# Attention into hash-routed experts on one core: where the token list stands, how rows are written, and which engine builds the tables

## The chip, the cores and the metric

The kernel runs on one core of a Trainium2 chip. The core has five engines that run their own instruction streams in order and meet through semaphores: PE (TensorE, matrix products), DVE (VectorE), ACT (ScalarE), POOL (GpSimd) and SP (SyncE, which here only sends DMAs). The metric is device time in microseconds (us), lower is better; three runs of the kernel before gave 185.52, 185.73 and 187.29, median 185.73.

## The reference, cut to what matters

Two blocks follow each other. The first is attention with polynomial features, for 4 batches, 4 heads, 1088 positions and head size 32:

```python
def phi(x):                      # S1, S2: 8 x 32
    a = np.einsum('rd,bhsd->bhsr', S1, x)
    b = np.einsum('rd,bhsd->bhsr', S2, x)
    return np.einsum('bhsi,bhsj->bhsij', a, b).reshape(*x.shape[:-1], 64)
q_p, k_p = phi(q), phi(k)
kv  = np.einsum('bhsf,bhsd->bhfd', k_p, v)
z   = np.sum(k_p, axis=2)
x   = einsum(q_p, kv) / (einsum(q_p, z) + 1e-6)    # -> 4352 tokens x 128
```

The second sends every token to one of 8 experts by its id, `token_ids * 2654435761 % 8`, and computes `relu(x @ w1[e]) @ w2[e]` with w1 of 128 x 1024 and w2 of 1024 x 128.

## The kernel before

**Order.** All five engines run in the order in which the program issues work (line 92). So where a call stands in the source is where its instructions stand on each engine, and an engine that waits holds up what is queued behind it.

**Attention.** Each of the four batches goes through the same steps. PE turns k and q (`turned_all`, L451 to L465; ACT copies the result out), multiplies them with the sketch matrices (`s_products`), ACT copies the first factors (`first_copied`), and DVE multiplies out the 64 features of q and of k (`features`, L510, two halves of four position tiles each). PE turns the features of q (`q_turned`, L559; ACT and DVE copy two quarters each), sums kv over the positions (`kv_products`, L532: eight tiles of 128 positions and a tail of 64), ACT copies it into a block diagonal m (`kv_diagonal`), and PE multiplies turned features with m (`x_products`, `x_tail_products`). A column of ones beside v gives the denominator. DVE inverts it (`denominators`), POOL scales the rows (`x_main`, `x_tail`, L597 to L612) and a DMA writes them to the DRAM tensor `x_rows`, in one piece of 512 KB for the main part and one of 32 KB for the tail. v is copied into place by POOL (`values`). The loop over b (L756) handles the products of batch b together with the features of batch b + 1; the fourth batch's products follow the loop (L812 to L821).

**Routing.** Between these steps the routing is spread out. DVE finds each token's expert, its rank among that expert's tokens and the expert's place in an order by size. `route_slots` (L365) turns that into a slot for each token, and splits the slot number into a tile number and a row number (st). `route_rows` and `route_tiles` (L403 to L411) build one-hot tables by comparing st with counters; `route_tiles_p` scales one of them on ACT. `route_list` (L416) is 34 products on PE that give, for each slot, the token in it, and `route_end` (L432) makes the two index tables, get for fetching and put for storing. In the third batch (b = 2) the list stands after kv, and the end after the products with the sketch matrices.

**Experts.** Each expert has two groups of slots: an early one of 256 tokens from the first two batches (groups 0 to 7) and a late one of 320 down to 271 columns (groups 8 to 15). `fetch_tile` (L665) gathers 128 rows by an indirect DMA of POOL; `paced` (L672) puts a small copy of the indices on DVE in front of it, so that it is not issued early. Chunks 0 and 1 are turned on PE (`bring`, L683). Later ones are split by DVE into halves of 16 bits (`turn_in`, L690), transposed by a DMA of SP, and put together again by DVE (`join_in`, L698). A group is eight products of the first layer (`layer1`, L831, four PSUM banks in turn, ACT clears the even ones and DVE the odd ones) interleaved with the eight of the second layer (`layer2`, L840) of the group before. At full speed it takes PE about 6.9 us for 256 columns. Results leave by ACT's copies, transposing DMAs (`turn_out`), DVE's joins (`join_out`) and indirect stores of POOL (`scatter`). The last group is handled in two parts, and its rows are turned on PE (`out_rows`).

**Work beside the products.** A list written out by hand (`beside`, L953 to L994) says after which product (group, chunk of the hidden layer) which of these steps is issued: `at(g, c, f, ...)`. The weights of the expert of rank r are loaded by `load_expert` (L132), on SP's queue; a tiny write into the target by ACT or DVE (`ahead`) holds the DMA back until that engine gets there. Weights of ranks 2 to 7 are sent at (0, 1), (1, 5), (2, 5), ... (5, 5).

## Time and profile before

| what | value |
|---|---|
| median of three runs | 185.73 us |
| the profiled execution | 188.05 us |
| its span | 186.3 us |
| PE busy | 174.3 us, 94% of the span |
| DVE, ACT, POOL busy | 98.1, 64.3, 94.9 us |
| mean granted clock of PE | 0.991 |
| DMA | 25.96 MB, mean 139 GB/s |

The profiled execution includes 1.75 us around its span. The attention stage runs from the start to about 56 us, the expert stage from there to the end; the chain that ended last consists of the last store and its DMA. PE's busy time overlaps from one product to the next, so it is best read by starts: two rows of the timeline with the same count tell how long a product takes at full speed. The timeline gives start, duration, engine, line, operation, output and inputs, the number of instructions merged, and in brackets the idle time before it and what ended it. "issue" there means that the engine waited for nothing that the profile shows.

### The profile page before, as it was taken

The page shows a single profiled execution, that of the slowest core. Times are in us where ns is not written, and L with a number is a line of the kernel's source. Part 1 is how long each engine was busy: PE and PEld are TensorE (multiplying, and loading weights), DVE is VectorE, ACT ScalarE, POOL GpSimd, SP SyncE. Part 2 cuts the span into 40 slices and gives each one's busy share as a digit, 9 for nine tenths or more (in the row PEclk, how much of TensorE's full clock was granted, in tenths as well). Part 3 has the DMA queues.
Part 4 walks back from the last instruction along what each step waited for, and adds up shares of the span by engine and source line. Part 5 has one row for each costly group of instructions (what it writes and reads, how often), then busy time and mean ns, then how long its engine had stood idle before and what let it go on. Part 6 is the DMA issues. An engine that isn't in the chain of part 4 may idle for free. (4 is left out here: it accounts for less than half of the span.)

```text
span 186.3 us, 4264 instructions
## 1 busy us (share of the span) xinstructions
PE 174.3 (94%) x1567; PEld 146.1 (78%) x1567; DVE 98.1 (53%) x302; ACT 64.3 (35%) x172; POOL 94.9 (51%) x130
## 2 busy tenths in 40 slices
PE   6989999999879999979999999999999999999880
PEld 1988979999677888858888887777777777778770
DVE  4688899999604453434553552633356463342230
ACT  3437674755224232322322332314133232321120
POOL 7253006080884585857648566445664640607642
PEclk9999999999978999999999999999999999999999
DMA  4994588707831969999799334142231512211101
GB/s 144 290 224 115 165 249 278 234 19 220 254 140 41 272 176 283 257 195 223 202 227 276 71 74 99 42 99 65 63 74 44 126 37 62 70 33 41 56 7 31
DMA packets 38406, 25.96 MB, mean 139 GB/s; under 512 B 21188, under 2 KB 35717, under 8 KB 38384
## 3 DMA queue, kind: packets, MB, share of 16 engines
q1 hardware_dynamic: 35808, 20.56, 43.3%
q0 software_dynamic: 2416, 5.08, 10.8%
q8 instruction: 13, 0.21, 0.5%
q14 instruction: 9, 0.07, 0.1%
q10 hardware_dynamic: 160, 0.04, 0.1%
HBM read 17.41 MB, written 4.52 MB: 118 GB/s over the span
## 5 line engine op out<-in xcount | busy, mean ns | idle before, releaser
L844 PE MATMUL op<-hT,w 128*128 128x256 f32 (+8 forms) x256 | 77.1, 390 | 0.7 <-issue 0.7
L624 DVE TENSOR_SCALAR hT<-hp 128x256 f32<-128x256 f32 (+9 forms) x68 | 29.0, 427 | 56.4 <-PE hp L836 32.8
L844 PEld LDWEIGHTS op<-hT,w 128*128 128x128 f32 x256 | 47.6, 190 | 11.8 <-issue 1.3
L847 POOL DMA_INDIRECT out_dram<-os,put x35 | 35.5, 1015 | 40.1 <-DVE os L905 21.2
L622 ACT ACTIVATE hT<-hp 128x256 f32<-128x256 f32 (+9 forms) x68 | 26.3, 390 | 67.0 <-PE hp L836 52.5
L836 PE MATMUL hp<-xT_late,w 128*128 128x320 f32 (+8 forms) x144 | 41.9, 386 | 0.0
L616 POOL DMA_INDIRECT xg<-x_rows,idx x31 | 31.6, 1019 | 16.3 <-issue 7.1
L836 PE MATMUL hp<-xT,w 128*128 128x256 f32 x128 | 37.5, 383 | 1.3 <-issue 1.3
L836 PEld LDWEIGHTS hp<-xT_late,w 128*128 128x128 f32 x144 | 25.4, 190 | 6.8
L836 PEld LDWEIGHTS hp<-xT,w 128*128 128x128 f32 x128 | 24.2, 192 | 5.3 <-issue 1.7
L601 POOL TENSOR_TENSOR xs<-xe,den 128x512 f32<-128x512 f32 x8 | 9.3, 1179 | 15.5 <-DVE den L595 15.4
L510 DVE TENSOR_TENSOR kp<-first_of_ab,ab_ps 128x1024 f32<-128x1024 f32 x8 | 9.5, 1196 | 1.2 <-ACT first_of_ab L503 1.2
L905 DVE COPY os<-turned 128x256 uint16<-128x256 uint16 (+1 forms) x26 | 7.9, 329 | 3.2 <-DMA turned<-half 1.7
L510 DVE TENSOR_TENSOR f<-first_of_ab,ab_ps 128x1024 f32<-128x1024 f32 x8 | 9.4, 1217 | 0.3 <-ACT first_of_ab L503 0.3
L575 PE MATMUL x_ps<-m,fT 128*64 128x66 f32 x256 | 9.4, 239 | 0.0
L575 PEld LDWEIGHTS x_ps<-m,fT 128*64 128x64 f32 x256 | 9.0, 153 | 0.2 <-ACT m L548 0.2
L539 PE MATMUL kv<-va,kp 128*64 128x33 f32 x256 | 8.6, 224 | 0.4 <-issue 0.4
L539 PEld LDWEIGHTS kv<-va,kp 128*64 128x64 f32 x256 | 8.1, 138 | 1.1 <-issue 1.0
L556 PE MATMUL fT_ps<-ident,f 128*128 128x128 f32 x64 | 8.3, 278 | 0.4 <-DVE f L510 0.2
L556 PEld LDWEIGHTS fT_ps<-ident,f 128*128 128x128 f32 x64 | 6.9, 141 | 1.3 <-DVE f L510 0.4
L884 ACT COPY half<-op 128x256 uint16<-128x256 uint16 x16 | 5.2, 375 | 7.3 <-PE op L844 6.4
L695 DVE COPY xh<-xg 128x256 uint16<-128x256 uint16 (+1 forms) x28 | 7.7, 315 | 0.0
(183 smaller groups left out, 161.7 us busy)
## 6 DMA issues: line engine op xcount, KB each, us to landing
w<-in_moe_w_dram SPq DMA_DIRECT2D x16, 512.0 KB
q<-in_q_dram SPq DMA_DIRECT2D x4, 512.0 KB
v<-in_v_dram SPq DMA_DIRECT2D x4, 512.0 KB
k<-in_k_dram SPq DMA_DIRECT2D x3, 512.0 KB
x_rows<-xs SPq DMA_DIRECT2D x3, 512.0 KB
out_dram<-os,put POOLq DMA_INDIRECT x35
k<-in_k_dram SPq DMA_DIRECT2D x2, 256.0 KB
x_rows<-xs POOLq DMA_DIRECT2D x1, 512.0 KB
```

Of the source, the lines that this page charges most:

```text
L510: nc.vector.tensor_tensor(dst[:].rearrange("p t h i j -> p (t h) i j")[:, r], a[:, r].unsqueeze(3).to_broadcast(shape), rows_of_ab(ab)[:, ...
L539: nc.tensor.matmul(kv[h * R * R:(h + 1) * R * R, pr], f[:, 2 * pr + h].rearrange("p i j -> p (i j)"), v_[:, 2 * pr + h], start=(t == 0 and ...
L556: nc.tensor.transpose(p[:, t, pr], f[:, 2 * i + t, 2 * pr:2 * pr + 2].rearrange("p h i j -> p (h i j)"), ident[:])
L575: nc.tensor.matmul(p[r, t, 2 * pr:2 * pr + 2].rearrange("p h d -> p (h d)"), fT[:, lo + t, pr, r], m[:, pr].rearrange("p h d -> p (h d)"), ...
L601: eng.tensor_tensor(rows_of[b][:, r], xes[b % 2][:, r, 0:D], dens[b][:, r].unsqueeze(2).to_broadcast([P, Q * H, D]), op=OP.mult)
L616: nc.gpsimd.indirect_dma_start(out=dst, out_offset=None, in_=x_dram[0:rows], in_offset=bass.IndirectOffsetOnAxis(ap=idx, axis=0), bounds_c ...
L622: nc.scalar.activation(dst, src, AF.Relu if relu else AF.Copy)
L624: return nc.vector.tensor_scalar(dst, src, 0.0, None, op0=OP.max).ins
L836: nc.tensor.matmul(hp[:, 0:hi - lo], w1[:, g % E, c * P:(c + 1) * P], x_columns(first_of(g) + lo, first_of(g) + hi), start=True, stop=True)
L844: nc.tensor.matmul(ops[g][:, 0:hi - lo], w2[:, g % E, c], hTs[g][:, c, lo:hi], start=(c == 0), stop=(c == FC - 1))
L847: st_ = nc.gpsimd.indirect_dma_start(out=out[:], out_offset=bass.IndirectOffsetOnAxis(ap=idx, axis=0), in_=src, in_offset=None, bounds_che ...
L905: nc.vector.tensor_copy(_half(os[:].rearrange("p a b -> p (a b)"), x)[:, 0:n * DM], tts[x][:, 0:n].rearrange("p a b -> p (a b)"))
```

## The change

- The order of loads at the start: the tails of q go ahead of the second batch's k.
- `route_slots`: its second part, nine operations, runs on POOL; two of DVE's combined operations become two on POOL.
- The multiplication and the scaling of the one-hot tables move from DVE and ACT to POOL; both, and both halves of the row table, are issued in the second batch (b = 1), ahead of the features.
- In the third batch q is turned before the features, the token list and its end stand between these transposes and kv, and only chunk 0 is fetched in the loop. Features of k are no longer split by the denominators.
- Rows of x are written in two parts, each as soon as it is scaled, with 2 KB instead of 4 KB in one piece per partition.
- Weights of ranks 0 and 1 are sent about one batch earlier (w2 of rank 1 after the fourth batch's kv). Rank 2 goes at (0, 4), and ranks 3 to 7 on ACT's own DMA queue at (1, 2) to (5, 2) without the tiny write.
- Chunk 0 is turned on PE in the middle of the fourth batch's kv; the fourth batch's x products and denominators stand after the second product of group 0. Chunk 1 is fetched after kv, and chunk 2 at (0, 3) and (0, 5). Chunk 1 is turned at (0, 6).
- Chunks 3 and 4 are fetched in group 1, chunks 5 and 6 in group 2 (before: 3 in group 0, 4 and 5 in group 1, 6 in group 2).
- The scaling of the third batch's rows moves from the loop to group 1, that of the fourth from group 1 to group 2, both with POOL's own DMAs.
- In the last group the last-but-one turn of rows stands after the fifth product instead of the third.

```diff
-    def load_expert(r, layers=(1, 2), ahead=None):
+    def load_expert(r, layers=(1, 2), ahead=None, eng=nc.sync, eng_type=ENG.SP):
...
-            nc.sync.dma_start(w1[:, r], moe_w1[bass.ds(e, 1)].rearrange("o p f -> p (o f)"))
+            eng.dma_start(w1[:, r], moe_w1[bass.ds(e, 1)].rearrange("o p f -> p (o f)"))
...
     k_tail = load_tail(k, "k_tail")
+    q_tail = load_tail(q, "q_tail")
     k_t.append(load_main(k, 1, "k"))
-    q_tail = load_tail(q, "q_tail")
...
         V_.scalar_tensor_tensor(pos[:], place_t[:], float(GD), pos[:], op0=OP.mult, op1=OP.add)
-        V_.tensor_scalar(over[:], pos[:], float(GL), 0.0, op0=OP.subtract, op1=OP.max)
-        V_.scalar_tensor_tensor(slot[:], over[:], float(2 * ST * P), slot[:], op0=OP.mult, op1=OP.add)
+        G_ = nc.gpsimd
+        G_.tensor_scalar(over[:], pos[:], float(GL), 0.0, op0=OP.subtract, op1=OP.max)
+        G_.tensor_scalar(over[:], over[:], float(2 * ST * P), None, op0=OP.mult)
+        G_.tensor_tensor(slot[:], slot[:], over[:], op=OP.add)
         st_f = const.tile([P, 2, C], F32, name="st_f")
...
+        G_.tensor_scalar(st_f[:, 1], st_f[:, 0], -float(P), None, op0=OP.mult)
+        G_.tensor_tensor(st_f[:, 1], st_f[:, 1], slot[:], op=OP.add)
+        G_.tensor_copy(st[:].rearrange("p k c x -> p (k c) x"),
...
     def route_tiles():
         hot(in_tile[:], number[:, 0:SE], st[:, 0])
-        nc.vector.tensor_tensor(tiles[:, :, 1].rearrange("p c (n x) -> p c n x", x=2),
+        nc.gpsimd.tensor_tensor(tiles[:, :, 1].rearrange("p c (n x) -> p c n x", x=2),
...
     def route_tiles_p():
-        nc.scalar.activation(tiles[:, :, 0], in_tile[:], AF.Copy, scale=p1[:])
+        nc.gpsimd.tensor_scalar(tiles[:, :, 0], in_tile[:], p1[:], None, op0=OP.mult)
...
-        if g == GQ - 1:
-            dma.dma_start(x_dram[b * S:b * S + SM].rearrange("(p t) d -> p (t d)", t=T),
-                          rows_of[b][:].rearrange("p n d -> p (n d)"))
+        dma.dma_start(x_dram[b * S:b * S + SM].rearrange("(p t) d -> p t d", t=T)[:, g * Q:(g + 1) * Q],
+                      rows_of[b][:, r].rearrange("p (t h) d -> p t (h d)", h=H))
...
-    for b in range(EB + 1):
+    for b in range(B - 1):
+        last = b == B - 2
         if b > 0:
             kT = turned_all(k_t[b + 1], "kT")
-            if b == 2:
-                load_expert(0, (2,), A.memzero)
+        if last:
+            qT = turned_all(q_t[b + 1], "qT")
         fT = q_turned(f, EVICT)
-        if b > 0:
-            qT = turned_all(q_t[b + 1], "qT")
...
-        if b == 2:
-            route_tiles_p()
+        elif not last:
+            qT = turned_all(q_t[b + 1], "qT")
+        if last:
+            idx = route_list()
+            route_end(idx)
         kv = kv_products(b, kp, range(T if b == 0 else 0, T + 1), kv if b == 0 else None)
-        if b == 2:
-            idx = route_list()
-        if b == 1:
-            v_t.append(load_main(v, 3, "v", A.memzero))
-            load_expert(0, (1,))
...
         if b == 1:
+            v_t.append(load_main(v, 3, "v", A.memzero))
+            load_expert(0, (1,))
             route_rows(0)
             route_tiles()
-        if b == 2:
-            route_end(idx)
-            for g in range(2):
-                for j in range(tiles_of(g)[1]):
-                    fetch_tile(g, j, True)
+            route_tiles_p()
+            route_rows(1)
         features(f, aq, abq, range(GQ))
...
-        if b == 2:
-            load_expert(1, (1, 2), A.memzero)
-        features(kp, ak, abk, [0])
-        denominators(b)
-        features(kp, ak, abk, [1])
         if b == 1:
-            route_rows(1)
-        for g in range(GQ):
-            x_main(b, g, nc.gpsimd)
-        x_tail(b, nc.gpsimd)
+            load_expert(0, (2,), A.memzero)
+            load_expert(1, (1,))
+        if b > 0:
+            features(kp, ak, abk, range(GQ))
+            denominators(b)
+        else:
+            denominators(b)
+            features(kp, ak, abk, range(GQ))
+        if not last:
+            for g in range(GQ):
+                x_main(b, g, nc.gpsimd)
+            x_tail(b, nc.gpsimd)
+        if last:
+            for j in range(tiles_of(0)[1]):
+                fetch_tile(0, j, True)
...
     fT = q_turned(f, EVICT)
-    kv = kv_products(e, kp, range(T + 1))
-    m = kv_diagonal(e, kv)
+    kv = kv_products(e, kp, range(T // 2))
+    bring(0, o_bank)
+    kv = kv_products(e, kp, range(T // 2, T + 1), kv)
+    load_expert(1, (2,), A.memzero)
+    last_m = kv_diagonal(e, kv)
     for j in range(2):
-        fetch_tile(2, j)
-    bring(0, o_bank)
-    x_products(e, fT, m)
-    x_tail_products(e, m)
-    denominators(e)
+        fetch_tile(1, j)
...
-    at(0, 3, bring, 1)
+    x3 = 1
+    at(0, x3, x_products, e, fT, last_m)
+    at(0, x3, x_tail_products, e, last_m)
+    at(0, x3, denominators, e)
+    for c in range(2):
+        at(0, 3 + 2 * c, fetch_tile, 2, c)
+    at(0, 4, load_expert, 2, (1, 2), lambda x: nc.vector.memset(x, 0.0))
+    at(0, 6, bring, 1, o_bank)
+    for g in range(1, E - 2):
+        at(g, 2, load_expert, g + 2, (1, 2), None, nc.scalar, ENG.Activation)
...
-    for g, n in enumerate((2, 4, 2, 2, 2, 2, 2, 2)):
+    for g, n in enumerate((0, 4, 4, 2, 2, 2, 2, 2)):
...
-    for g in range(E - 2):
-        at(g, 1 if g == 0 else 5, load_expert, g + 2, (1, 2), lambda x: nc.vector.memset(x, 0.0))
-    for g in range(GQ):
-        at(1, 6, x_main, e, g, nc.gpsimd, nc.gpsimd)
-    at(1, 7, x_tail, e, nc.gpsimd, nc.gpsimd)
+    for b, g in ((B - 2, 1), (e, 2)):
+        for i in range(GQ):
+            at(g, 5, x_main, b, i, nc.gpsimd, nc.gpsimd)
+        at(g, 6, x_tail, b, nc.gpsimd, nc.gpsimd)
...
-        if c == 2:
+        if c == 4:
             out_rows(mid, ST - 1 - mid)
```

## The prediction

> **What bounds the kernel now.** I read the page first, then PE's timeline by the place where its stream is broken, then what ends each break.
>
> ```profile
> span 186.3 us, 4264 instructions
> PE 174.3 (94%) x1567; PEld 146.1 (78%) x1567; DVE 98.1 (53%) x302; ACT 64.3 (35%) x172; POOL 94.9 (51%) x130
> PEclk9999999999978999999999999999999999999999
> ```
>
> PE is the bound: 94% busy, no other engine above 53%. A change can gain only where PE is idle or slow. The clock row dips once, in the twelfth and thirteenth slices (51 to 61 us). PE's timeline there:
>
> ```profile
> 47.42 2.22 PE L539 MATMUL kv<-va,kp 128*64 128x33 f32 x61
> ...
> 50.77 0.38 PE L539 MATMUL kv<-va_tail,f_tail 128*64 128x33 f32 x6 [0.41 <-issue]
> 51.53 0.24 PE L539 MATMUL kv<-va_tail,f_tail 128*64 128x33 f32 x1 [0.38 <-issue]
> 52.46 0.54 PE L687 MATMUL xp<-ident,xg 128*128 128x128 f32 x2 [0.69 <-DMA xg<-x_rows,get]
> 52.99 3.30 PE L575 MATMUL x_ps<-m,fT 128*64 128x66 f32 x64
> 56.08 0.65 PE L584 MATMUL x_ps<-m,fT_tail 128*64 128x66 f32 x4
> 56.66 2.14 PE L836 MATMUL hp<-xT,w 128*128 128x256 f32 x8
> ...
> 58.86 2.66 PE L836 MATMUL hp<-xT,w 128*128 128x256 f32 x10
> 61.35 0.59 PE L844 MATMUL op<-hT,w 128*128 128x256 f32 x2
> ```
>
> PE is idle 1.87 us in four pieces (0.39, 0.41, 0.38, 0.69), the last of them a wait for the first gathered rows. Then it runs at half clock:
>
> ```profile
> 55.00:56.00 1.00, 1.00 (x24) 1.00 (x21) 0.00 (x0) 0.05 (x1) 0.69 (x2) 0.50 0.86 336
> ```
>
> (stretch; length; busy time of PE, PEld, DVE, ACT, POOL; granted clock 0.50; DMA share, GB/s). The same 64 x products go from 43.32 to 45.20 at full clock, 1.88 us; here they take 3.09. Full-clock starts elsewhere give: 16 transposes of f 1.89, kv 1.89 and its tail 0.33, x 1.88 and its tail 0.33, two transposes of rows 0.35, a layer product with 256 columns 0.43. From the fourth batch's first transpose (45.53) to the first second-layer product (61.35) PE has 1.89 + 2.22 + 0.35 + 2.21 + 9 x 0.43 + 0.35 = 10.9 us of work in 15.8. **So 4.9 us can be won here**, and little elsewhere. What sets the end of the wait is POOL's chain:
>
> ```profile
> 37.73 3.10 POOL L601 TENSOR_TENSOR xs<-xe,den 128x512 f32<-128x512 f32 x2 [6.75 <-DVE den L595]
> 40.79 0.39 POOL L610 TENSOR_TENSOR xs_tail<-xe,den 64x128 f32<-64x128 f32 x1
> 46.47 1.28 POOL L616 DMA_INDIRECT xg<-x_rows,get  x1 [4.31 <-issue]
> 48.06 0.99 POOL L616 DMA_INDIRECT xg<-x_rows,get  x1 [0.30 <-issue]
> ```
>
> Gathers need the second batch's rows in DRAM: scaled by 40.83, gather begun 5.64 later, second gather issued at 49.05, PE released at 52.46.
>
> **The change, part by part.**
>
> 1. *Slots to GpSimd (batch 0).* DVE loses the nine operations from 21.96 to 23.44: 1.48 us. On POOL, nine small ones by the rows of the order's table (L343 to L348, one each 0.36 to 0.53): about 3.7, from 21.95 to 25.6, in a stretch where POOL idles 8.69. Queued behind them is the second batch's v (1.05): 26.7, needed at 27.2. So nothing on PE; if the small ones took 0.6 each, PE would wait about 1. DVE's features end 1.5 earlier, which ends PE's short waits at 24.7 (0.16, and about 0.4 of stretch): **-0.5**.
>
> 2. *Tile table to GpSimd (batch 1).* On DVE the multiplication took 0.80, on ACT the scaling 1.33. No POOL row has 1224 bf16 elements; the nearest are scaling rows, 1.03 for 512 f32 with two inputs (2.46 by size), and the copy of 1024 with one (1.03, so 1.23). A floor is ACT's and DVE's own 2.1 for the pair, a ceiling the two-input rate with 50% for sharing, 3.7 each, 7.4. I take 2.5 + 1.4. There is sharing:
>
> ```profile
> 29.63 2.50 DVE L399 TENSOR_TENSOR row<-number,st 128x2176 bf16<-128x2176 bf16 x1
> 38.58 1.35 DVE L399 TENSOR_TENSOR row<-number,st 128x2176 bf16<-128x2176 bf16 x1
> ```
>
> The same operation takes 2.50 while POOL copies v, and 1.35 at 38.58, where POOL's second scaling took 2.06 and not 1.03: one of the two is held up. With both row halves and the comparison on DVE ahead of features, DVE ends the second half at about 33.5 (28.5, held to 31.4, +0.8, +1.35) and POOL's pair then ends at 37.4. Features run 33.5 to 38.2, denominators to 38.8, scaling to 40.9: **no gain on POOL's chain** (before: 40.83). The list on PE, now due at 37.3, waits 0 to 1.3 for POOL's pair; I take 0.3.
> [...]
>
> 3. *List ahead of kv, one chunk at once, weights early.* The list's 1.2 us of PE only change place. Its six DVE operations (1.5) end at 41.5, before rows have landed, so the list is not what releases the gathers; the rows are. Their path shortens: half of them are sent 1 us earlier, and the weights, which were queued on SP at 42.01 right behind the tail, go out around 35. The stretch from scaling to gather (5.64) becomes 3.5 to 5.6, taken 4.1 (half the bytes, 0.8 less, and no weights behind): gather at 45.0, its pair issued at 47.6. Last landing took 3.4 under 1 MB of weights; without, those of a gather issued by 139.04 moved from 139.75 to 140.0, so 1.0 at least; between 1.0 and 3.4 I take 2.3: **rows at 49.9** (48.0 with both low ends, 52.5 with both high ones).
>
> 4. *Kv split around the first chunk.* PE gets there at 45.53 - 0.5 + 0.3 + 1.89 + 0.95 = 48.1, so it waits 1.8 (0 to 4.4). After that 10.9 - 2.84 = 8.06 of work, since two first-layer products cover m's copy (two of 0.21) and the x products' copies lie beside products. Add 0.15, as the second chunk's copy (0.41) has one product of 0.43 behind it. First second-layer product at 58.1, against 61.35: **-3.25**, of which parts 1 and 2 are already inside. Should the half clock return, it costs 1.65 (3.3 us at half).
> Before, 1.4 us idle inside the 3.4 before 53.8 brought it; 1.28 at 81.8 did not. A wait of 1.8 stands close. [...]
>
> 5. *Third chunk later.* Before, its gathers were issued by 56.92, 4.5 us ahead of DVE's split at 61.46. Now they stand at the fourth and sixth products of group 0, behind the denominators, issued by about 58.7, landed at 61.0, while DVE reaches the split at 58.9. Queued behind the split: evictions (four banks cover 1.7), the next four index copies and their gathers. Split, transposing DMA (at most 4.1 from issue to use in group 1) and join (0.5) end at 66.2; group 2 needs it at 58.1 + 6.9 = 65.0: **+1.1** (0 to 2.5).
>
> 6. *Weights of ranks 3 to 7 on ACT's queue.* Two issues a group; ACT's own two took 0.59 and 0.36. ACT is busy a third, and an eviction of 0.38 queues behind; four banks cover it: nothing, at worst 0.3 a group. SP is freed of the same issues, its transposes no longer stand behind 1 MB, but share engines with it.
>
> 7. *Deferred scalings.* POOL gets, in groups 1 and 2, each four gathers (1.3 with gap), three operations (2.45) and three sends (0.93 with gap): 10.4, and group 2 two scatters (2.6): 23.4 in 13.8 us. It catches up at 5.2 a group of 6.9. First late chunk is due in group 4: enough. Nothing, unless DMA is full (rival 3).
>
> 8. *Tail.* PE waits once near the end:
>
> ```profile
> 177.92 0.41 PE L912 MATMUL tp<-ident,late_cols 128*128 128x128 f32 x2 [0.53 <-ACT late_cols L886]
> ```
>
> With two more products ahead of the transposes this wait is covered, the scatters start no later, the last products end 0.5 earlier: **-0.5**. The earlier q_tail ends a 0.39 wait at 13.89, but the next batch's k comes later: zero, 0.4 either way.
>
> Sum: -3.25 + 1.1 - 0.5 = -2.65. The profiled execution took 188.05 (span 186.3 and 1.75 around); 185.4 by that. It lies 2.3 above the median of 185.73, so I carry the difference to the median: **183.1**.
>
> **Rivals.**
>
> *Rival 2, the wait moves with its half clock.* Rows land 50.5 or later, PE waits 2.4 or more, the clock halves: -3.25 + 0.6 + 1.65, third chunk +0.5 (PE comes to it later), tail -0.5: -1.0, 184.7. For it: 1.4 us idle sufficed once. Against: no weights travel then.
>
> *Rival 3, slower.* One mechanism: turned chunks land after their group begins, in groups 2 to 5. It happened once:
>
> ```profile
> 82.47 0.51 DVE L701 COPY xT<-xh_turned 128x256 uint16<-128x256 uint16 x2 [2.35 <-DMA xh_turned<-xh]
> ```
>
> DVE waited 2.35 and PE lost 1.28 at 81.8. Groups 1 to 3 now carry 1 MB of weights each, two batches' rows and twice the gathers, where the DMA share was already about 1.0 from 67.5 to 75. It decides once a landing is over 2.2 us past its join's slot. Four groups at 1.28, and 1.0 more for the third chunk: +6.1 on -2.65 is +3.45; less the one such stall of before, 1.28: +2.2, 187.9. Against: weights no longer stand ahead of transposes on one queue.
>
> *Rival 4, no list effect:* POOL's pair takes 7.4; list and scaling come 3.5 later, gathers too: 186.6 without, 188.2 with the half clock; counted with rival 3 or within 1%.
>
> **How the numbers follow.** Forecast 0.46, rival 2 0.30, rival 3 0.18, rival 4 0.06. If rows are there when PE comes and the third chunk costs half, -5.05 + 0.55 - 0.5 gives 180.7. The range goes from there to 187.7, which leaves out rival 3's upper part and the end of rival 4. A change of 1% (1.86) is about what a measurement can tell from none: faster 0.46, same 0.33, slower 0.21.
>
> **What would show it.** In the changed kernel: PE's wait at the first rows' transposes (1.8) and granted clock after it (1.00); the first second-layer product about 3 us earlier; DVE's wait at the split of the third chunk (2); POOL's two table operations (2.5 and 1.4); no wait of the list over 0.5. Wrong if gathers begin at 46.5 as before, if the clock halves, or if joins wait in groups 2 to 5.

## The result, and the profile after

The changed kernel is slower: median 195.56 us of four runs (193.92 to 197.32), the kernel before 186.01 beside it; the ratio is 1.0473 (95% interval 1.038 to 1.0566). An execution more than 1.5% above the fastest of its kernel counts as slow, and the ratios compare the others alone. The forecast was 183.1 with a range of 180.7 to 187.7. The profiled execution took 195.57 us, 7.5 us longer than that of before. The lines of its page that answer to those of before:

```profile
span 193.8 us, 4260 instructions
PE 173.5 (90%) x1567; PEld 144.6 (75%) x1567; DVE 102.1 (53%) x291; ACT 63.2 (33%) x171; POOL 106.6 (55%) x145
PEclk9999999999999979999997999999999999999999
```

PE is busy as long as before, but 90% instead of 94% of a longer span. The dip of the clock has left the twelfth and thirteenth slices; two new ones stand in slices 15 and 22 (68 to 73 and 102 to 107 us), inside the expert groups. PE's timeline, from the list to the sixth group:

```profile
38.99 1.26 PE L421 MATMUL idx_ps<-tiles,row 128*128 128x72 bf16 x34 [1.30 <-POOL tiles L416]
...
49.57 0.44 PE L688 MATMUL xp<-ident,xg 128*128 128x128 f32 x2
52.29 2.10 PE L577 MATMUL x_ps<-m,fT 128*64 128x66 f32 x64
58.26 0.59 PE L845 MATMUL op<-hT,w 128*128 128x256 f32 x2
69.44 0.70 PE L837 MATMUL hp<-xT,w 128*128 128x256 f32 x2 [3.85 <-DVE xT L702]
82.23 0.70 PE L837 MATMUL hp<-xT,w 128*128 128x256 f32 x2 [1.35 <-DVE hT L625]
88.94 0.70 PE L837 MATMUL hp<-xT,w 128*128 128x256 f32 x2 [2.12 <-DVE xT L702]
100.64 1.11 PE L837 MATMUL hp<-xT,w 128*128 128x256 f32 x2 [1.94 <-DVE hT L625]
```

Up to 58.26 this execution does what was forecast: the first chunk is turned without a wait, the x products run at full clock (2.10 where they took 3.30), and the first second-layer product starts 3.09 us earlier than before (61.35). Then come four waits of more than 1 us, for joined chunks (xT) and for evictions (hT, copies of products out of PSUM), where before had one of 1.28. After the first, PE runs at half clock:

```profile
71.00:72.00 1.00, 1.00 (x3) 0.74 (x3) 0.57 (x3) 0.00 (x0) 0.63 (x3) 0.50 0.18 70
```

(columns as in the row of 55 to 56 us before; 0.50 is the granted clock.) POOL's timeline, the tables and the first gathers:

```profile
32.33 3.23 POOL L411 TENSOR_TENSOR tiles<-in_tile,twice 128x1224 bf16<-128x1224 bf16 x1 [0.73 <-DVE in_tile L401]
35.55 3.39 POOL L416 TENSOR_SCALAR tiles<-in_tile,p 128x1224 bf16<-128x1224 bf16 x1
...
44.85 1.29 POOL L617 DMA_INDIRECT xg<-x_rows,get  x1 [1.92 <-issue]
46.44 1.01 POOL L617 DMA_INDIRECT xg<-x_rows,get  x1 [0.30 <-issue]
```

**Where the time went, in one table.** PE's first second-layer product of each group marks the groups; an interval is the time from one mark to the next. A group of 256 columns that nothing holds up takes 6.91 us in every kernel here, and from the seventh mark to the sixteenth all twenty profiled executions need 68.83 us to 0.01. So a kernel is described by the first mark, the six intervals after it (floor 6 x 6.91 = 41.46) and what follows. All rows are single profiled executions.

| kernel | first mark | the six intervals | over the floor |
|---|---|---|---|
| before | 61.35 | 6.91 6.91 8.43 6.91 6.91 6.91 | 1.5 |
| after | 58.26 | 11.71 8.59 10.91 6.91 10.80 6.91 | 14.4 |

From before to after the first mark gives -3.1 and the intervals +12.9. What follows the seventh mark takes 82.0 us to the span's end in before and 79.7 in after: -2.3, and the sum is the +7.5 of the spans. That last term is no gain of the change. It goes by the chip on which a profile was taken: 79.2 to 79.8 in the eight profiles of the third and fourth set below, 81.5 to 84.3 in the ten of the others, with the old tail or the new.

The third chunk is the first to be late. In the lines, a split is DVE's copy xh<-xg, a join its copy xT<-xh_turned or os<-turned, and ACTq and SPq are the DMA queues of ACT and SP. All engines' timelines of the changed kernel, the lines that concern it:

```profile
60.88 0.35 ACTq L143 DMA_DIRECT2D w<-in_moe_w_dram  x1
61.39 0.41 ACTq L147 DMA_DIRECT2D w<-in_moe_w_dram  x1
61.85 0.49 DVE L696 COPY xh<-xg 128x256 uint16<-128x256 uint16 x2 [3.76 <-DMA xg<-x_rows,idx]
62.51 10.10 SPq L697 DMA_TRANSPOSE xh_turned<-xh  x2
67.29 2.09 DVE L702 COPY xT<-xh_turned 128x256 uint16<-128x256 uint16 x2 [3.40 <-DMA xh_turned<-xh]
67.95 1.06 POOL L603 TENSOR_TENSOR xs<-xe,den 128x512 f32<-128x512 f32 x1
69.62 1.77 DVE L696 COPY xh<-xg 128x256 uint16<-128x256 uint16 x2
```

Its rows come late (3.76 us of DVE's wait), its transposes go out 1.1 us behind a megabyte of weights on the other queue and are there for the join 4.8 us after their issue, and the join takes 2.09 us instead of 0.5 beside POOL's scaling. Three of the change's moves meet here: the weights on ACT's queue, the later gathers, and the deferral, that is the later scaling of two batches' rows. The experiments take them apart.

### The profile page after: what moved, and what is told of

Its sections match the earlier page's. It is cut to its first block, busy times and chain, and to the rows that moved or that the text cites. A ratio compares the mean times of both kernels' runs of the same rounds, so it can differ in the third digit from the quotient of the medians.

```text
span 193.8 us, 4260 instructions
## 1 busy us (share of the span) xinstructions
PE 173.5 (90%) x1567; PEld 144.6 (75%) x1567; DVE 102.1 (53%) x291; ACT 63.2 (33%) x171; POOL 106.6 (55%) x145
## 3 DMA queue, kind: packets, MB, share of 16 engines
q0 software_dynamic: 2624, 5.64, 10.2%
## 5 line engine op out<-in xcount | busy, mean ns | idle before, releaser
L845 PE MATMUL op<-hT,w 128*128 128x256 f32 (+8 forms) x256 | 78.2, 396 | 0.0
L845 PEld LDWEIGHTS op<-hT,w 128*128 128x128 f32 x256 | 48.6, 194 | 11.1
L837 PE MATMUL hp<-xT,w 128*128 128x256 f32 x128 | 39.9, 401 | 9.8 <-DVE xT L702 6.0
L617 POOL DMA_INDIRECT xg<-x_rows,idx x33 | 33.7, 1020 | 23.1 <-DVE idx L677 11.2
L906 DVE COPY os<-turned 128x256 uint16<-128x256 uint16 (+1 forms) x26 | 8.6, 358 | 9.1 <-DMA turned<-half 8.8
L696 DVE COPY xh<-xg 128x256 uint16<-128x256 uint16 (+1 forms) x28 | 9.0, 362 | 3.8 <-DMA xg<-x_rows,idx 3.8
L603 POOL TENSOR_TENSOR xs<-xe,den 128x512 f32<-128x512 f32 x8 | 8.3, 1055 | 0.7 <-DVE den L597 0.6
L702 DVE COPY xT<-xh_turned 128x256 uint16<-128x256 uint16 x12 | 4.9, 458 | 6.8 <-DMA xh_turned<-xh 6.6
L577 PE MATMUL x_ps<-m,fT 128*64 128x66 f32 x256 | 8.3, 222 | 0.0
L577 PEld LDWEIGHTS x_ps<-m,fT 128*64 128x64 f32 x256 | 7.9, 137 | 0.3 <-issue 0.3
```

Of the source, the lines that this page charges most:

```text
L577: nc.tensor.matmul(p[r, t, 2 * pr:2 * pr + 2].rearrange("p h d -> p (h d)"), fT[:, lo + t, pr, r], m[:, pr].rearrange("p h d -> p (h d)"), ...
L603: eng.tensor_tensor(rows_of[b][:, r], xes[b % 2][:, r, 0:D], dens[b][:, r].unsqueeze(2).to_broadcast([P, Q * H, D]), op=OP.mult)
L617: nc.gpsimd.indirect_dma_start(out=dst, out_offset=None, in_=x_dram[0:rows], in_offset=bass.IndirectOffsetOnAxis(ap=idx, axis=0), bounds_c ...
L696: nc.vector.tensor_copy(xh[:, x * w:(x + 1) * w], _half(xg3[k][:].rearrange("p a b -> p (a b)")[:, 0:w], x))
L837: nc.tensor.matmul(hp[:, 0:hi - lo], w1[:, g % E, c * P:(c + 1) * P], x_columns(first_of(g) + lo, first_of(g) + hi), start=True, stop=True)
L845: nc.tensor.matmul(ops[g][:, 0:hi - lo], w2[:, g % E, c], hTs[g][:, c, lo:hi], start=(c == 0), stop=(c == FC - 1))
```

## The experiments

The runs come in five sets. Runs of one set stand on one chip, and each ratio is against the kernel before on that chip. It took 188.65, 189.16, 185.54, 185.80 and 188.48 us in the five sets, so ratios are compared, not times, and best inside a set.

### First set: one suspect put back at a time

Theory W: weights on ACT's queue at the third product. Theory G: the third chunk gathered too late. **a1_w_sp5** puts the weights back on SP:

```diff
-        at(g, 2, load_expert, g + 2, (1, 2), None, nc.scalar, ENG.Activation)
+        at(g, 5, load_expert, g + 2, (1, 2), lambda x: nc.vector.memset(x, 0.0))
```

> The changed kernel, but the weights of ranks 3 to 7 go as before: on SP's queue, at the sixth product of groups 1 to 5, behind a tiny write of DVE. Theory W (the weights, sent on a second queue at the third product, travel beside the transposing DMAs and make DVE's joins late): PE's waits of 1.35, 2.12 and 1.94 us in groups 3 to 5 go and the one in group 2 (3.85 and the half clock behind it) shrinks to some 2: 187 to 190 us against 195.6 of the changed kernel. Theory G (the third chunk is gathered too late, and the rest is a late train behind it): the weights don't matter, 194 to 196.

**a2_w_act5** moves them to the sixth product, still on ACT's queue:

```diff
-        at(g, 2, load_expert, g + 2, (1, 2), None, nc.scalar, ENG.Activation)
+        at(g, 5, load_expert, g + 2, (1, 2), None, nc.scalar, ENG.Activation)
```

> The changed kernel with the weights of ranks 3 to 7 still on ACT's queue, but issued at the sixth product of groups 1 to 5 instead of the third. It separates the two halves of theory W: if the place in the group counts, the time is that of the run with SP's queue (187 to 190 us); if the second queue counts, because its transfers interleave with the transposes wherever they are issued, it stays at 194 to 196. Theory G: 194 to 196 as well.

**a3_chunk2** gathers the third chunk behind the second, ahead of the first group:

```diff
     for j in range(2):
         fetch_tile(1, j)
+    for j in range(2):
+        fetch_tile(2, j)
...
-    for c in range(2):
-        at(0, 3 + 2 * c, fetch_tile, 2, c)
```

> The changed kernel, but the third chunk is gathered right behind the second one, ahead of group 0, as before the change. Theory G: DVE's wait of 3.76 us at its split, PE's wait of 3.85 us ahead of group 2 and the half clock behind it (1.65) go: 189 to 191 us. Theory W: the chunk comes in time, but its transposes still travel beside 1 MB of weights: 193 to 195 us, PE's waits in groups 3 to 5 as they were.

**a4_w_sp5_chunk2** does what a1 and a3 do.

> Both of these together: the weights of ranks 3 to 7 on SP's queue at the sixth product and the third chunk gathered ahead of group 0. If the two are independent causes of PE's waits, all of them go and the 3.1 us won ahead of the expert stage remain: 183 to 185 us, faster than both kernels. If the deferred scaling of two batches' rows on GpSimd is what makes things late, it stays at 188 or more.

Measured: a1 1.036 (two executions of 195.25 and 195.52 against 188.65 us, so without an interval; two more took 198.33 and 200.27), a2 1.0727 (1.0647 to 1.0807), a3 1.0567 (1.045 to 1.0684), a4 1.0347 (1.0274 to 1.042). Neither a1 nor a3 brings what its theory promised, and a4, for which 183 to 185 us was expected of two independent causes, stays 3.5% above before. Neither theory carries the loss alone, and in a4 the third chunk's late join is gone (first interval 6.91) while the fifth interval takes 13.33. So a third cause, or a second sufficient one, is in what a4 leaves: the front, the deferral and the later gathers. On a2, its trace answers the question that it was to decide. At the sixth product the megabyte goes out on ACT's queue at 63.63 and 64.15, around the third chunk's transposes (63.93), and DVE joins them 6.77 us after their issue, where the changed kernel needed 4.78: a later place on that queue does not help.

### Second set: each move alone, and the front alone

**b1_scale2** puts the third batch's scaling back ahead of the first group, behind the second chunk's gathers:

```diff
     for j in range(2):
         fetch_tile(1, j)
+    for g in range(GQ):
+        x_main(B - 2, g, nc.gpsimd)
+    x_tail(B - 2, nc.gpsimd)
...
-    for b, g in ((B - 2, 1), (e, 2)):
+    for b, g in ((e, 2),):
```

> The changed kernel with one thing put back: the third batch's rows are scaled on GpSimd ahead of the first group, behind the second chunk's gathers, and go out on SP's queue; the last batch stays at the third group. Theory D (two batches of scaled rows with six sends of their own on GpSimd's queue, in the first two full groups, push the gathers of the fourth to sixth chunk back and crowd the DMA there): half of it goes, some 4 us of the 9.5 lost, so 1.02 to 1.03 of the kernel before, and PE's wait for the fourth chunk (88.94 us, 2.1) goes. Theory R (the front itself costs the expert groups: the last batch's products, their evictions and the second chunk's turning now stand inside the first group, beside its loads): 1.04 to 1.05, unchanged.

**b2_before_defer** is the kernel before with the deferral alone (in the loop, x_main and x_tail only for b < 2; rows of the last two batches in two parts):

```diff
-    for g in range(GQ):
-        at(1, 6, x_main, e, g, nc.gpsimd, nc.gpsimd)
-    at(1, 7, x_tail, e, nc.gpsimd, nc.gpsimd)
+    for b, g in ((B - 2, 1), (e, 2)):
+        for i in range(GQ):
+            at(g, 5, x_main, b, i, nc.gpsimd, nc.gpsimd)
+        at(g, 6, x_tail, b, nc.gpsimd, nc.gpsimd)
```

> The kernel before with the deferral alone: the third batch's rows are scaled at the second group's sixth product and the last batch's at the third group's, in two parts and a tail each, sent on GpSimd's queue; gathers, weights and front as before. Theory D: 1.02 to 1.04, with waits for turned chunks in the second to fourth group. Theory R: 0.99 to 1.01.

**b3_front** is b1 with weights as in a1, the third chunk gathered behind the scaling, two, four and two gathers in the first three groups, and the last batch scaled at (1, 6) and (1, 7): the new front, the old groups.

> The changed kernel's front (slots and tables on GpSimd, list ahead of kv, first chunk turned inside the last kv, last batch's products in the first group) with the expert groups of the kernel before: the third batch scaled ahead of the first group, the third chunk gathered ahead of it, two gathers in the first group, the last batch scaled at the second group's seventh product, weights on SP at the sixth. Theory D: the 3.1 us of the front stay, 0.98 to 0.99. Theory R: the groups lose as before, 1.02 to 1.04, with waits of PE at joins in the second and third group.

**b4_before_wact** is the kernel before with the changed kernel's line for the weights:

```diff
-    for g in range(E - 2):
-        at(g, 1 if g == 0 else 5, load_expert, g + 2, (1, 2), lambda x: nc.vector.memset(x, 0.0))
+    at(0, 1, load_expert, 2, (1, 2), lambda x: nc.vector.memset(x, 0.0))
+    for g in range(1, E - 2):
+        at(g, 2, load_expert, g + 2, (1, 2), None, nc.scalar, ENG.Activation)
```

> The kernel before with the weights of the fourth to eighth expert issued on ACT's queue at the third product, nothing else. Theories D and R: within 1% (0.99 to 1.01), since ten issues of 0.35 to 0.5 us on an engine that is busy a third of the time hold nothing up. If the weights' place matters by itself: 1.02 or more, by joins that wait for transposed chunks behind them.

Measured: b1 1.0489 (1.0371 to 1.0608), b2 1.0425 (1.0341 to 1.0508), b3 0.9974 (0.9923 to 1.0025), b4 1.0283 (1.019 to 1.0376). Theory R (the front costs the groups) falls with b3: without the three moves the loss is gone. Theory D falls by half with b1: the third batch's scaling put back helps nothing while the weights stay on ACT's queue and the gathers late. And b4 refutes what both theories and the forecast said of the weights: alone, in the old kernel, they cost 2.8%. But b2's rows show no late join. They show something else, which comes back below.

### Third set: queue or place, one batch or the other, and the tail

**c1_before_wsp2** keeps SP and the memset and changes the place alone:

```diff
-        at(g, 1 if g == 0 else 5, load_expert, g + 2, (1, 2), lambda x: nc.vector.memset(x, 0.0))
+        at(g, 1 if g == 0 else 2, load_expert, g + 2, (1, 2), lambda x: nc.vector.memset(x, 0.0))
```

> The kernel before with the weights of the fourth to eighth expert at the third product in place of the sixth, still on SP and still behind a memset. Theory place (their 1 MB per group runs beside the transposes of the next chunk, issued around the group's first product and joined at its sixth, so the join waits): as with ACT's queue, 1.02 to 1.035, waits of PE for joins of 1 to 2 us in several groups. Theory queue (a second hardware queue shares the 16 DMA engines with the transposes, while on one queue they follow each other): 0.99 to 1.01.

**c2_before_defer4** defers the last batch alone:

```diff
-        at(1, 6, x_main, e, g, nc.gpsimd, nc.gpsimd)
-    at(1, 7, x_tail, e, nc.gpsimd, nc.gpsimd)
+        at(2, 5, x_main, e, g, nc.gpsimd, nc.gpsimd)
+    at(2, 6, x_tail, e, nc.gpsimd, nc.gpsimd)
```

> The kernel before with the last batch's scaling and sends alone deferred, from the second group's seventh product to the third group's sixth; the third batch stays ahead of the first group. If the last batch's lateness is what costs (its sends meet the scatters that begin in the third group): 1.02 to 1.04. If it is the third batch's (its scaling no longer stands between the gathers ahead of the first group, so that six of them run back to back, and its sends come into the second group): 0.995 to 1.01.

**d1_front_mid** is b3 with the third batch's scaling between the first chunk's gathers and the second's:

```diff
-        if not last:
-            for g in range(GQ):
-                x_main(b, g, nc.gpsimd)
-            x_tail(b, nc.gpsimd)
         if last:
             for j in range(tiles_of(0)[1]):
                 fetch_tile(0, j, True)
+        for g in range(GQ):
+            x_main(b, g, nc.gpsimd)
+        x_tail(b, nc.gpsimd)
...
-    for g in range(GQ):
-        x_main(B - 2, g, nc.gpsimd)
-    x_tail(B - 2, nc.gpsimd)
```

> The run with the changed front and the old expert groups (0.997), with the third batch's scaling moved up between the first chunk's gathers and the second's, where GpSimd idled for 3.7 us; the third chunk's gathers follow the second's at once. If GpSimd's order around 50 to 56 us held up the copy of m (it started at 53.8 us, 1.5 us after the last kv product, where the changed kernel had it at 51.3): 0.975 to 0.99, first second-layer product at 58 to 58.5 us. If six gathers back to back hold it up wherever they stand: 0.995 to 1.005, with m late by 1 us or more.

**c3_before_tail** has the changed tail alone:

```diff
-        if c == 2:
+        if c == 4:
             out_rows(mid, ST - 1 - mid)
```

> The kernel before with the last group's second transposes and scatters at its fifth product in place of the third. By the prediction's term: 0.5 us less, 0.997 (0.992 to 1.002). Its profile also shows the middle of the kernel before on this chip: the wait of 1.28 us at 83.1 us for which no releaser was shown.

Measured: c1 1.0075 (1.0009 to 1.0141), c2 1.0096 (1.0035 to 1.0157), d1 0.9965 (0.9903 to 1.0027), c3 1.0045 (0.9995 to 1.0096). The place of the weights costs 0.75%; on ACT's queue the same place cost 2.8% (b4, on another chip). The tail gives nothing here. d1's profile has the forecast's front and almost no waits behind it (table below), though its time is not clearly under the kernel before.

How the queue costs is seen in the same group of b4 and c1, in the timelines of all engines. First b4, weights on ACT's queue:

```profile
70.59 2.49 SPq L897 DMA_TRANSPOSE turned<-half  x2
71.53 0.35 ACTq L143 DMA_DIRECT2D w<-in_moe_w_dram  x1
72.05 0.49 ACTq L147 DMA_DIRECT2D w<-in_moe_w_dram  x1
79.44 0.31 DVE L905 COPY os<-turned 128x256 uint16<-128x256 uint16 x1 [4.76 <-DMA turned<-half]
80.12 0.70 PE L836 MATMUL hp<-xT,w 128*128 128x256 f32 x2 [1.78 <-DVE hT L624]
```

Then c1, the same product, on SP's queue:

```profile
70.97 3.02 SPq L897 DMA_TRANSPOSE turned<-half  x2
71.16 0.06 DVE L971 MEMSET w<- 128x1 f32 x1
74.86 0.36 SPq L143 DMA_DIRECT2D w<-in_moe_w_dram  x1
75.86 0.31 DVE L905 COPY os<-turned 128x256 uint16<-128x256 uint16 x1 [1.24 <-DMA turned<-half]
```

The memset frees c1's weights at 71.2, when ACT's were issued, but on SP they stand behind the transposes and go out at 74.86. So in these rows the queue also sets when they leave, 3.3 us apart. On ACT's queue they go out in the midst of the transposes, and the second turned half is there at 79.44 instead of 75.86. DVE meanwhile stands on the join (4.76 us), PSUM evictions stand behind the join on DVE, and PE stops for one of them (1.78). From the transposes' issue to the join of the second half it is 8.85 us in b4 and 4.89 in c1. How the DMA engines serve two queues at a time no row shows.

### Fourth set: d1 as base, one move added at a time

With d1's front and groups as base, the changed kernel is d1 plus three moves. Each is added alone. **f1_wact** adds the weights:

```diff
-        at(g, 5, load_expert, g + 2, (1, 2), lambda x: nc.vector.memset(x, 0.0))
+        at(g, 2, load_expert, g + 2, (1, 2), None, nc.scalar, ENG.Activation)
```

> The changed front with the old expert groups (third batch scaled between the first two chunks' gathers), and on it the weights of the fourth to eighth expert on ACT's queue at the third product. If ACT's queue is a cause by itself (theory queue: two hardware queues' transfers interleave, so the transposes of the next chunk end later than its group's sixth product): 1.02 to 1.03 of the kernel before, PE waiting for joins. If only together with the others: 0.99 to 1.0.

**f2_defer** adds the deferral (the third batch out of the loop, both batches in the groups):

```diff
-    for i in range(GQ):
-        at(1, 6, x_main, e, i, nc.gpsimd, nc.gpsimd)
-    at(1, 7, x_tail, e, nc.gpsimd, nc.gpsimd)
+    for b, g in ((B - 2, 1), (e, 2)):
+        for i in range(GQ):
+            at(g, 5, x_main, b, i, nc.gpsimd, nc.gpsimd)
+        at(g, 6, x_tail, b, nc.gpsimd, nc.gpsimd)
```

> The same base with the third batch's scaling at the second group's sixth product and the last batch's at the third group's, sent on GpSimd's queue. If the deferral is a cause by itself (10 us of scaling and sends in GpSimd's line ahead of the gathers of later chunks and of the scatters): 1.015 to 1.035. If only together with the later gathers: 0.995 to 1.005.

**f3_late** adds the later gathers:

```diff
-    for j in range(2):
-        fetch_tile(2, j)
...
+    for c in range(2):
+        at(0, 3 + 2 * c, fetch_tile, 2, c)
...
-    for g, n in enumerate((2, 4, 2, 2, 2, 2, 2, 2)):
+    for g, n in enumerate((0, 4, 4, 2, 2, 2, 2, 2)):
```

> The same base with the gathers of the third chunk at the first group's fourth and sixth product, of the fourth and fifth in the second group, of the sixth and seventh in the third. The changed kernel waited 3.76 us for the third chunk's rows, 3.85 on PE and ran 3.3 us at half clock behind it. If that comes from the place of the gathers alone: 1.015 to 1.03, with that one stall at the second group's end and none later. If it comes from what else shares the DMA engines there: 0.99 to 1.0.

**f4_tables** takes the two table operations of d1 back to DVE and ACT:

```diff
-        nc.gpsimd.tensor_tensor(tiles[:, :, 1].rearrange("p c (n x) -> p c n x", x=2),
+        nc.vector.tensor_tensor(tiles[:, :, 1].rearrange("p c (n x) -> p c n x", x=2),
...
-        nc.gpsimd.tensor_scalar(tiles[:, :, 0], in_tile[:], p1[:], None, op0=OP.mult)
+        nc.scalar.activation(tiles[:, :, 0], in_tile[:], AF.Copy, scale=p1[:])
```

> The same base with the token tables on DVE and ACT again, slots still on GpSimd. The list waited 1.3 us for GpSimd's tables in the changed kernel; with the two tables at 0.8 and 1.5 us on DVE and ACT the list starts up to 1.3 us earlier, but the third batch's feature products and copies start later by as much as DVE and ACT spend: 0.990 to 1.000 of the kernel before, within 0.5 us of the base.

Measured: f1 1.0138 (1.0057 to 1.0219), f2 0.9886 (0.982 to 0.9952), f3 0.9977 (0.9922 to 1.0032), f4 0.992 (0.9879 to 0.9961). The base d1 had 0.9965 on another chip; against it f1 costs 1.7%, f3 0.1%, and f2 nothing. Against f4 on the same chip, which also has the tables back, f1 costs 2.2% and f3 0.6%. Added up, the three make 1.0 to 2.5%, where the changed kernel stands 5.1% above d1's ratio.

### Fifth set: two moves at once

**g1_wact_late** is d1 with f1's and f3's edits, without the deferral.

> The changed front and the old groups with two of the three moves: weights on ACT's queue at the third product, and the gathers a group later; the scaling of the two batches stays early. If weights and late gathers act together (the third chunk's transposes, late by 4 us, now stand in the stretch where the fourth expert's megabyte comes in): 1.03 to 1.05, with the stall of 3 to 4 us of PE and the half clock at the second group's end as in the changed kernel. If they only add up: 1.015 to 1.025.

**g2_defer_late** is d1 with f2's and f3's edits, which is a1 again.

> The other pair: the two batches' scaling deferred and the gathers a group later, weights on SP at the sixth product behind a memset. If deferral and gathers act together (in the second and third group GpSimd has four gathers, two scalings, three sends and then scatters in a line): 1.025 to 1.045, as in the first experiment's 1.044. If ACT's queue is needed for the loss: 0.99 to 1.005.

Measured: g1 1.0448 (1.0349 to 1.0548), g2 1.0465 (1.033 to 1.0601). Both pairs cost about as much as all three moves, on a chip where the kernel before takes 188.5. In g2 and a1, which are one kernel measured on two chips (1.0465 and 1.036), nothing goes on ACT's queue: that queue is not needed for a loss of nearly this size. The third pair, weights and deferral on d1's front, was not run. The pairs ran on chips on which the kernel before takes 188.5 us and more, the single moves of the fourth set on one with 185.8, so what the pairing adds is not separated from the chip. The marks of all kernels that tell the moves apart:

| kernel | first mark | the six intervals | over the floor |
|---|---|---|---|
| d1, base | 58.51 | 6.91 7.29 7.72 6.91 6.91 6.91 | 1.2 |
| f1, weights | 62.02 | 6.91 6.91 10.41 6.91 10.01 6.91 | 6.6 |
| f2, deferral | 63.59 | 6.91 7.18 7.93 7.77 6.91 7.98 | 3.2 |
| f3, gathers | 58.72 | 8.22 9.89 8.51 6.91 6.91 6.91 | 5.9 |
| f4, tables back | 60.92 | 6.91 6.91 7.07 6.91 6.91 6.91 | 0.2 |
| g1, weights and gathers | 60.73 | 10.46 6.91 10.82 6.91 9.46 6.91 | 10.0 |
| a1, deferral and gathers | 59.69 | 8.39 7.68 10.26 8.01 10.80 7.08 | 10.8 |
| g2, the same kernel | 59.39 | 8.45 10.42 9.15 6.91 13.64 6.96 | 14.1 |
| b4, before and weights | 62.20 | 6.91 6.91 10.48 7.95 10.08 6.91 | 7.8 |
| b2, before and deferral | 63.87 | 6.91 6.91 8.02 7.47 13.55 6.99 | 8.4 |
| c1, before, place only | 62.15 | 6.91 6.91 7.98 6.91 6.91 6.91 | 1.1 |

The executions of f1, f2, f3 and g2 in this table took 191.40, 189.62, 187.34 and 198.92 us, above their medians of 188.92, 182.96, 185.85 and 198.72: their intervals tell which wait stands where, not what a move costs on the whole. The first mark varies too: a1, a2 and g2, whose instructions up to it are those of the changed kernel, have it at 59.69, 59.29 and 59.39.

So most of the loss is placed. **The third and fifth interval** (10.91 and 10.80 in the changed kernel): ACT's queue alone is enough for them. f1 and b4 have them at 10.4 to 10.5 and 10.0 to 10.1, g1 at 10.8 and 9.5, and f3 and c1 do not. But it is not the only way to them: a1, with the weights on SP, has 10.26 and 10.80. Its lines in the third interval:

```profile
76.23 0.35 SPq L143 DMA_DIRECT2D w<-in_moe_w_dram  x1
76.78 1.18 SPq L147 DMA_DIRECT2D w<-in_moe_w_dram  x1
78.07 1.67 SPq L697 DMA_TRANSPOSE xh_turned<-xh  x1
84.42 0.51 DVE L702 COPY xT<-xh_turned 128x256 uint16<-128x256 uint16 x2 [2.70 <-DMA xh_turned<-xh]
85.03 1.19 PE L837 MATMUL hp<-xT,w 128*128 128x256 f32 x2 [2.46 <-issue]
```

Here the chunk's transposes stand 1.3 us behind the megabyte on the one queue, and DVE joins them 6.35 us after their issue; in g2 it is 6.90, and in the kernel before the transposes of 76.37, behind weights of 73.88 and 74.43, were joined after 6.10 (PE's wait of 1.28 ends with that join). In these rows one queue keeps a transpose quick only where it is issued ahead of the weights: a1's chunk before this one, issued at 71.39 and so ahead of those of 76.23, was joined after 3.23. The waits in a1's fifth interval (0.98 and 1.34 us of PE) have no releaser in the trace. **The first interval** (11.71) needs two moves: gathers alone make 8.22 (with the deferral 8.4), weights alone 6.91, both 10.46. In f3's timelines the same chunk, as late as in the changed kernel, has its transposes to itself:

```profile
62.58 0.49 DVE L696 COPY xh<-xg 128x256 uint16<-128x256 uint16 x2 [4.03 <-DMA xg<-x_rows,idx]
63.13 1.33 SPq L697 DMA_TRANSPOSE xh_turned<-xh  x1
65.69 0.64 DVE L702 COPY xT<-xh_turned 128x256 uint16<-128x256 uint16 x2 [1.06 <-DMA xh_turned<-xh]
70.04 1.88 DVE L696 COPY xh<-xg 128x256 uint16<-128x256 uint16 x2 [3.39 <-DMA xg<-x_rows,idx]
72.31 0.70 PE L836 MATMUL hp<-xT,w 128*128 128x256 f32 x2 [1.31 <-DVE idx L677]
```

2.56 us from transposing to join, where the changed kernel needed 4.78 and lost 3.85 on PE and then the half clock. f3's own price is the next chunk, whose rows are 3.39 late. The changed kernel stands above g1 in the first two intervals by 1.25 and 1.68, the second being the half clock behind its longer wait. The two differ by the deferral, and the join of 2.09 and the split of 1.77 beside POOL's scaling fit that, but they ran on different chips.

A version that beats both kernels is f2: new front, weights on SP, early gathers, and both batches' scaling deferred, 182.96 us where the kernel before took 185.80, 0.9886 (0.982 to 0.9952). It is a gain of 1.1% on one chip, in four of five executions; the fifth took 189.62. f4's edit with it was not tried.

## Why the prediction was wrong

**The front was right in this execution, in part by luck.** Gathers began at 44.85 (forecast 45.0), PE turned the first chunk at 49.57 (49.9), the first second-layer product came at 58.26 (58.1): -3.09 against -3.25, at full clock. On the way there terms were off and cancelled. Step 1 claimed 0.5 us and gave 0.33: from the first batch's transposes of f (17.27) to the second's (25.01) PE needs 7.73 to 7.75 us in every changed front, and 8.07 in before. But PE had come to that stretch 0.62 later, and the fourth batch's first transposes came at 46.62, 1.09 later than before. Step 2 took 2.5 and 1.4 for the tables on POOL; they took 3.23 and 3.39, 6.62 together, near the ceiling of 7.4, and the list waited 1.30 instead of 0.3. The ceiling came from the row that is alike in kind (two inputs, shared); the choice of 1.4 for the scaling leant on a copy. PE therefore came 1.5 us later than the 48.1 of step 4, and the rows were there: its wait of 1.8 did not occur. In a1 and a2, the same instructions up to the first mark, PE instead waited 1.51 and 1.49 us for the copy of m ahead of the x products, which step 4 held to be covered. Rival 2 did not happen in the changed kernel. It did in the profiled execution of f2, where the second gather came late:

```profile
51.87 0.33 PE L688 MATMUL xp<-ident,xg 128*128 128x128 f32 x1 [1.34 <-DMA xg<-x_rows,get]
...
56.23 3.48 PE L577 MATMUL x_ps<-m,fT 128*64 128x66 f32 x64
```

The clock there falls from 1.00 to 0.50 between 52 and 53 us, behind one wait of 1.34 (3.48 for 64 products). But a1, a2, a4 and b1 waited 1.49 to 1.58 us ahead of the x products and kept full clock (64 products in 2.10; a4's in two stretches), and a3 fell to half behind 2.18 (3.48 again). So the length of one wait does not decide it, and whether the 1.8 of step 4 would have cost its 1.65 stays open.

**Step 6 failed, and it alone was enough to turn the sign.** It priced the weights on ACT's queue by ACT's time for issuing them, nothing to 0.3 a group. It counted as a relief that transposes "no longer stand behind 1 MB", and named the sharing of engines without a price (in the changed kernel, behind the issues of weights and transposes, the mean busy share of the 16 engines is 0.98 or more in every half microsecond from 63.0 to 66.5). What it left out is the other side of the one queue: there the weights of a group also stood behind that group's transposes (before: transposes at 70.18, weights at 73.88), which kept these quick (the second half joined after 5.04 us). On ACT's queue the megabyte goes beside them (b4: transposes at 70.59, weights at 71.53, the second half joined after 8.85). Alone that costs 1.7 to 2.8%, 3 to 5 us, against a forecast gain of 2.65 (f1 against d1 and f4; b4). In f1 it is 3.5 and 3.1 us over the floor in the two intervals where a turned half is joined late.

**Steps 5 and 7 failed as a pair.** They were priced singly, 1.1 and nothing, and f3 and f2 bear that out singly. Together, with the weights on SP, they cost 3.6% (a1) and 4.65% (g2). So step 6 is not the whole account: each of two pairs, both with the later gathers in them, is enough for most of the loss, by runs on other chips than the changed kernel's. What the second pair's loss consists of is shown for the third interval and open for the rest.

**Rival 3 is what happened, at about twice its price, and what it named as speaking against it was one of the causes.** It named turned chunks that land after their group begins, groups 2 to 5, four times 1.28 and 1.0 more, 6.1 us in the groups and 187.9 in all, with a chance of 0.18. The intervals grew by 12.9. The waits in the trace are 3.85 (then the half clock), 1.35, 2.12 and 1.94. Two of the four are not for a chunk but for evictions behind DVE's wait on an outgoing turned half, a consequence that the rival did not price.

**Step 5's term was mis-sized by four times.** The third chunk was to cost 1.1 (0 to 2.5); its interval is 4.80 over the floor, and the half clock behind it 1.68 in the next. Gathers issued by 58.78 and the split at 61.85 are close to the forecast (58.7, 61.0). The transposes were given 4.1 at most and took 4.78; the join was given 0.5 and took 2.09; and the half clock was not in the term at all. f3 shows the move alone at 1.3 in that interval, inside the forecast, and with step 6 it is 3.6 (g1). The later chunks, gathered later too, had no term of their own: f3's next two intervals are 3.0 and 1.6 over the floor.

**Step 7** said nothing for the deferral unless the DMA is full. As a move on the new front that held (f2, 0.9886); in the old kernel it cost 4.25% (b2), and with the later gathers 4.65% (g2), the latter two on chips on which the kernel before was slower as well. So it stands unsettled rather than right.

**Step 8** gave nothing (c3, 1.0045), not 0.5, but c3 could not show it: on its chip c1 and c2, with the old tail, do not have the wait of 0.53 either. b4, on another chip, has it (0.52); no run there makes this edit alone. The 2.3 us by which the profiled execution of before lay above its median are the longer stretch behind the seventh mark (82.0 against 79.2 to 79.8), which no edit moves; so to carry the difference to the median was right.

## What to carry to other kernels

Here a second hardware DMA queue was no free place for bulk loads: the weights on it cost 1.7 to 2.8% (f1, b4). On one queue, the small transfers that were issued first went ahead of the megabyte (a chunk in a1 was joined 3.23 us after their issue) and those issued after it waited for it (6.10 in before, 6.35 in a1); on two they went beside it (the second half joined 8.85 us after their issue in b4, against 4.89 on one queue in c1). Price a moved transfer by what it runs beside and by what waits for that, not by the time its engine takes to issue it. And where a move spends a transfer's slack (gathers a group later), every other move that draws on the same slack must be priced together with it: here the gathers and the deferral cost 0.6% or less singly, and 3.6 to 4.65% as a pair on other chips.

## What the runs showed of the hardware that was not expected

**DVE's copies stretch beside POOL's scaling.** Two copies of 128x256 that take 0.51 us together took 2.09, and the split 1.77 instead of 0.49 (f3: 1.88), each beside POOL's two-input operations of 1.06. In the changed kernel's single records the first copy of each pair starts while POOL still issues a DMA and ends 0.16 to 0.18 us after the scaling that follows it (67.29 to 69.18, scaling to 69.01; 69.62 to 71.19, scaling to 71.03). So each also spans what was left of that issue, and the growths of 1.3 to 1.6 us exceed one operation. What holds DVE up in that time no row shows.

**Engines that are idle beside finished products.** In b2, a4 and g2 the fifth interval takes 13.3 to 13.6 us without a late chunk. All engines' timelines of b2:

```profile
98.43 2.13 SPq L901 DMA_TRANSPOSE turned<-half  x2
99.28 1.04 POOL L619 DMA_INDIRECT xg<-x_rows,idx  x1 [0.30 <-issue]
100.63 1.01 POOL L619 DMA_INDIRECT xg<-x_rows,idx  x1 [0.31 <-issue]
102.04 0.38 ACT L625 ACTIVATE hT<-hp 128x256 f32<-128x256 f32 x1 [8.28 <-remote]
102.48 0.70 PE L840 MATMUL hp<-xT,w 128*128 128x256 f32 x2 [4.38 <-issue]
103.53 0.76 DVE L627 TENSOR_SCALAR hT<-hp 128x256 f32<-128x256 f32 x2 [6.65 <-PE hp L840]
```

PE's products before that were started by 97.5 at the usual pace, yet ACT clears the first of their banks at 102.04 after 8.28 us idle, and then all engines go on at once. POOL alone kept issuing gathers and stores, one each 1.35 us, since 85.8. All three kernels have the deferral, and all three ran on chips where the kernel before took 188.5 to 189.2; f2 and c2, on the other chips, do not have it. These two conditions are not enough: a2 and a3, with the deferral on such a chip, take 6.91 there, and a1, the kernel of g2, 10.80. Whether POOL's unbroken row of indirect DMAs causes it, and what it is that comes late, was not settled: no run here changes that row alone on such a chip.

**Chips differ by 1.5 to 2%.** The kernel before took 185.5 to 186.0 us in the third and fourth set and beside the changed kernel, and 188.5 to 189.2 in the others. In the profiles the difference stands in the last group: from the sixteenth mark to the span's end it is 10.3 to 11.0 us on the former chips, and 12.6 to 15.6 on the latter and in the profile of before, where PE also ends its products later (7.6 to 10.2 us after that mark instead of 5.9 to 6.1). The deferral cost 4.25% on one of the latter chips (b2) and nothing on one of the former (f2, though on the new front).
